# Two weight loads between the weightings of V, and V's last block weighted after all of them

## The chip, the cores and the metric

The kernel runs on one core of a Trainium2 chip. The metric is the device time of one execution in microseconds; lower is better. Three executions of the kernel before took 358.61 to 360.15 us, with a median of 359.97 us.

## What is computed

Eight batches of eight heads go through a causal attention whose scores decay with a running sum, and the result, rearranged to 4608 tokens of 512 numbers, goes through a normalised gated feed-forward layer:

```python
scores = scale * np.matmul(q, k.transpose(0, 1, 3, 2))
cum = np.cumsum(np.maximum(s, 0.0), axis=-1)
bias = -(cum[:, :, :, None] - cum[:, :, None, :])
scores = np.where(causal, -1000000000.0, scores + np.minimum(bias, 0.0))
attn = softmax(scores)                      # B, H, S, D = 8, 8, 576, 64
x = (attn @ v).transpose(0, 2, 1, 3).reshape(B * S, H * D)
xn = x / np.sqrt(np.mean(x * x, -1) + 1e-06) * rms_g
g, val = xn @ w_gate, xn @ w_val            # 512 x 1536 each
out = (g * sigmoid(g) * val) @ w_out        # 1536 x 512
```

## The kernel before

Everything is bf16 on TensorE (PE) with fp32 sums. A batch has 576 positions, in blocks of 128, 128, 128, 128 and 64. The feed-forward part works on nine chunks of 512 tokens. For each chunk, `ffn` (line 940) walks the 12 blocks of 128 hidden features, fb = 0 to 11: a product with `wg_sb` (line 957, here called G of block fb), one with `wv_sb` (line 967, V of block fb), ScalarE's tanh of G (line 960), two operations on VectorE (lines 970 and 962) that free the two PSUM banks again; then four blocks of tokens are multiplied by `wout_sb` (line 988). Between these products, `step` (line 855) deals out the attention of the next batches: transposes of K and Q (`t_step`, line 199, matmuls of line 203), scores (line 286), exponentials (lines 310 and 326), masks on GpSimd (line 319), the products with V (`av_step`, lines 437 and 443). Every engine executes its own instructions strictly in the order in which this code emits them; nothing reorders them later.

The change lies in the opening, written out by hand from line 1090 on, before the first chunk. There the attention of the first four blocks of batch 0 is done with nothing else beside it. The decay of batch 0 is folded into V: `fold_v` (line 415) multiplies one block of V by a number per row and head, on VectorE for block 1 and on GpSimd (POOL) for blocks 0, 2, 3 and 4. Block 4 of V is read by the last block's attention, which is dealt out only inside the first chunk.

The weights come in pieces by `load_w(src, dst, f0, f1)` (line 1007): a DMA that POOL issues, from fp32 in HBM to bf16 in SBUF, for the blocks f0 to f1-1. Before the change POOL issues them in this order: gate 0-3, val 0-1, then behind the three foldings val 2-5, after the last of the small normalisation operations (`alpha`, lines 474 and 477) gate 4-7 and val 6-11, and, out of the first chunk's steps, gate 8-11.

Two more things use the DMA engines and the same engines' queues at that time. `load1(g)` (line 1139) brings K and Q of batch 1 in fp32, four heads at a time: two DMAs of 512 KB each, issued by SyncE (SP), for heads 0-3 after the second block's attention and for heads 4-7 after the third's. They are turned into bf16 in pieces: K of heads 0-3 by four casts on VectorE (`piece1`, line 1255), Q of heads 0-3 by four on POOL (line 1253), K and Q of heads 4-7 half by POOL and half by ScalarE (lines 1265 to 1269). Only then can PE transpose them. The transposes stand in PE's order between the products of the first chunk: those of K, heads 0-3, ahead of G of block 2; the first of Q, heads 0-3, between G and V of block 2.

In the profile all weight loads have line 1009, all foldings on POOL line 417, the casts line 153 (POOL and VectorE) or 151 (ScalarE).

Of the kernel before, what the change touches and what calls it, by code (L numbers as in the profile page):

```python
# [26 lines left out]
def kernel(  # L27
# [34 lines left out]
    wg_sb = pers.tile([128, CC, DF], BF16, name="wg_sb")  # L62
    wv_sb = pers.tile([128, CC, DF], BF16, name="wv_sb")
# [45 lines left out]
    def psF():  # L109
        return pp.tile([128, DM], FP32, name="psF", tag="F", bufs=4)  # L110
# [304 lines left out]
    def fold_v(eng, c):  # L415

        eng.tensor_tensor(out=v_sb[:, 0, c], in0=v_sb[:, 0, c],
                          in1=vw[:, c, :].unsqueeze(2).to_broadcast([128, H, NV]), op=ALU.mult)
# [53 lines left out]
    def alpha(c0, c1, R=slice(0, 128)):  # L472

        nc.gpsimd.tensor_scalar(  # L474
            out=al_all[R, c0:c1], in0=ss_all[R, c0:c1],
            scalar1=1.0 / DM, scalar2=EPS, op0=ALU.mult, op1=ALU.add)
        nc.gpsimd.tensor_tensor(  # L477
            out=al_all[R, c0:c1], in0=al_all[R, c0:c1],
            in1=mhalf[R, 0:c1 - c0], op=ALU.pow)
# [369 lines left out]
    def warm(n):  # L849

        ps = psF()
        for i in range(n):
            nc.tensor.matmul(ps, lhsT=ident_bf, rhs=mneg, start=True, stop=True)
# [153 lines left out]
    def load_w(src, dst, f0, f1):  # L1007
        fs = slice(f0 * 128, f1 * 128)
        nc.gpsimd.dma_start(out=dst[:, :, fs],
                            in_=src[:, fs].rearrange("(cc p) f -> p cc f", p=128))  # L1010
# [79 lines left out]
    with tc.manual_schedule():  # L1090
# [32 lines left out]
        ACT, DVE, POOL = nc.scalar, nc.vector, nc.gpsimd  # L1123
# [4 lines left out]
        def pairF():  # L1128
            return (psF(), psF())

        def s_first(kb, g, pair=None):
            do_s((0, kb, g), pair)()
# [54 lines left out]
        s_first(2, 0)  # L1187
        fold_v(POOL, 0)
        load_w(moe_w_val, wv_sb, 0, 2)
        for c in (2, 3, 4):  # L1190
            fold_v(POOL, c)
        s_first(0, 1, pairF())
        tail_step(0, psAV16())
        fold_v(DVE, 1)
# [8 lines left out]
        norms += [do_av((0, 1, 1), psT32(), act=True, apart=True)]  # L1203
        norms[0](False)
        alpha(0, 1)
        load_w(moe_w_val, wv_sb, 2, 6)
        s_first(3, 1, pairF())
        norms[1](False)
        ps = psS()
# [13 lines left out]
        norms += [do_av((0, 3, 1), psT32(), act=True, apart=True)]  # L1223
        norms[3](False)
        alpha(3, 4)
        load_w(moe_w_gate, wg_sb, 4, 8)
        load_w(moe_w_val, wv_sb, 6, 12)
        warm(4)
        for qb in range(4):
            x_scale(0, qb, gq)  # L1230
# [253 lines left out]
```

## Time and profile before

| | |
|---|---|
| median of three executions | 359.97 us (358.61 to 360.15) |
| the profiled execution, its own time | 357.18 us |
| its span from first to last instruction | 355.7 us |
| granted TensorE clock over the span | 0.998 |
| PE busy | 343.4 us (97%) |
| VectorE (DVE) busy | 278.5 us (78%) |
| ScalarE (ACT) busy | 212.2 us (60%) |
| GpSimd (POOL) busy | 204.3 us (57%) |
| DMA, mean over the span | 128 GB/s |

Times in the rows of the trace are microseconds from the start of the span; the profiled execution's own time is 1.5 us more than the span. A row of the timeline has start, duration, engine, line, operation, what is written and read, and in brackets the idle time before it and what ended that. A row of the DMA view has the name of a queue, its packets, megabytes and the time that its packets took as a share of 16 engines over the window; queue q0 is that of the loads which POOL issues, q1 that of SP. A row of DMA issues ends with the microseconds from issue to landing.

### The profile page before, as it was taken

What the parts mean: (1) busy time and instruction counts of PE and PEld (TensorE: products, weight loads), DVE (VectorE), ACT (ScalarE), POOL (GpSimd) and SP (SyncE); (2) the same over time, 40 slices, a digit from 0 to 9 for tenths busy, and PEclk for the clock granted to TensorE, in tenths of its full rate; (3) what the DMA queues carried; (4) which work ended last, traced back from release to release, by engine and by line L of the source; (5) the groups of instructions that cost most, each with busy time, mean ns of one, the idle gap of its engine ahead of it and who ended that gap; (6) DMA issues with size and microseconds to landing.
All of it is one profiled execution on the core that took longest, in us unless ns stands there. A gap on an engine that the chain in (4) does not pass through costs nothing.

```text
span 355.7 us, 7020 instructions
## 1 busy us (share of the span) xinstructions
PE 343.4 (97%) x2461; PEld 167.4 (47%) x2461; DVE 278.5 (78%) x528; ACT 212.2 (60%) x467; POOL 204.3 (57%) x336
## 2 busy tenths in 40 slices
PE   5989999999999999999999999999999999999995
PEld 2465444544444444444454454444544554444443
DVE  6798889598967987798789886988798659836840
ACT  3977885878786546864577557654565445324322
POOL 6988564456669986687498988497735320000000
PEclk9999999999999999999999999999999999999999
DMA  7999999899959999999999999296810131020002
GB/s 217 145 241 235 172 178 260 188 192 199 92 122 170 147 149 155 166 206 181 154 150 132 79 151 198 38 105 103 153 24 17 46 104 23 2 88 29 2 32 92
DMA packets 130528, 45.68 MB, mean 128 GB/s; under 512 B 110548, under 2 KB 125656, under 8 KB 130488
## 3 DMA queue, kind: packets, MB, share of 16 engines
q0 software_dynamic: 67056, 13.70, 52.4%
q1 hardware_dynamic: 53792, 24.20, 35.4%
q10 hardware_dynamic: 9640, 7.29, 8.1%
q8 instruction: 20, 0.33, 0.5%
q14 instruction: 20, 0.16, 0.2%
HBM read 37.90 MB, written 9.44 MB: 133 GB/s over the span
## 4 chain that ended last, share of the span: by engine, by line
PE 77%; DMA 7%; POOL 4%; DVE 4%; ACT 3%; issue 3%; SPq 0%; POOLq 0%; DVEq 0%; ACTq 0%
PE psF L988 26%; PE psF L967 20%; PE psF L957 19%; DMA kqT<-kqn 4%; DMA wg_sb<-in_moe_w_gate_dram 3%; PE psAV L443 2%; PE psS L286 2%; PE psAV L437 2%; PE psF L367 1%; DVE U L970 1%; POOL v_sb L409 1%; PE psS L367 1%; DVE x_sb L453 1%; DVE Ht L962 1%; ACT E L326 1%
## 5 line engine op out<-in xcount | busy, mean ns | idle before, releaser
L957 PE MATMUL psF<-xnT,wg_sb 128*128 128x512 bf16 x424 | 108.9, 379 | 0.6 <-DMA wg_sb<-in_moe_w_gate_dram 0.5
L967 PE MATMUL psF<-xnT,wv_sb 128*128 128x512 bf16 x424 | 108.9, 379 | 0.4 <-DMA wv_sb<-in_moe_w_val_dram 0.4
L960 ACT ACTIVATE T<-psF 128x512 f32<-128x512 f32 x108 | 64.7, 599 | 64.5 <-PE psF L957 61.3
L988 PE MATMUL psF<-wout_sb,Ht 128*128 128x512 bf16 (+2 forms) x444 | 100.9, 374 | 0.0
L970 DVE SCALAR_TENSOR_TENSOR U<-T,psF 128x512 bf16<-128x512 f32 x108 | 73.6, 681 | 23.5 <-ACT T L960 23.1
L962 DVE TENSOR_TENSOR Ht<-U,psF 128x512 bf16<-128x512 bf16 x99 | 67.7, 684 | 6.8
L988 PEld LDWEIGHTS <-Ht 128*128 128x128 bf16 x444 | 40.1, 98 | 43.5 <-issue 1.4
L967 PEld LDWEIGHTS <-wv_sb 128*128 128x128 bf16 x424 | 38.9, 98 | 44.5 <-issue 2.9
L957 PEld LDWEIGHTS <-wg_sb 128*128 128x128 bf16 x424 | 38.6, 98 | 42.2 <-issue 1.9
L992 ACT ACTIVATE osb<-psF 128x512 f32<-128x512 f32 (+2 forms) x37 | 21.7, 586 | 59.5 <-PE psF L988 52.8
L384 POOL TENSOR_SCALAR_AFFINE_SELECT E<-E 128x512 bf16<-128x512 bf16 (+1 forms) x50 | 34.8, 704 | 29.5 <-ACT E L380 19.7
L194 POOL DMA_DIRECT2D v_sb<-in_v_dram x40 | 35.4, 885 | 0.2 <-issue 0.2
L484 DVE SCALAR_TENSOR_TENSOR xs_sb<-x_sb,al_all,g_row 128x512 bf16<-128x512 bf16 (+1 forms) x36 | 29.6, 821 | 4.1 <-POOL al_all L477 3.9
L310 ACT ACTIVATE E<-psS,biasK 128x256 bf16<-128x256 f32 (+3 forms) x88 | 29.3, 424 | 2.9 <-PE psS L286 2.9
L474 POOL TENSOR_SCALAR al_all<-ss_all 128x1 f32<-128x1 f32 (+2 forms) x39 | 11.5, 295 | 33.3 <-ACT xs_sb L461 26.9
L453 DVE TENSOR_TENSOR x_sb<-psAV,rZ 128x256 bf16<-128x256 f32 (+1 forms) x66 | 28.0, 424 | 2.3
L522 DVE TENSOR_TENSOR acc<-acc,mag 128x1280 bf16<-128x1280 bf16 x32 | 27.5, 878 | 0.2
L477 POOL TENSOR_TENSOR al_all<-al_all,mhalf 128x1 f32<-128x1 f32 (+2 forms) x39 | 25.2, 645 | 3.2
L443 PEld LDWEIGHTS <-E 128*128 128x128 bf16 x320 | 21.7, 98 | 10.5 <-POOL E L384 0.7
L409 POOL TENSOR_TENSOR v_sb<-v_sb,vwx 128x512 bf16<-128x512 bf16 x25 | 25.9, 1037 | 0.1
L461 ACT ACTIVATE xs_sb<-x_sb 128x512 bf16<-128x512 bf16 (+1 forms) x37 | 23.3, 629 | 4.3 <-DVE x_sb L453 3.7
L319 POOL TENSOR_SCALAR_AFFINE_SELECT E<-E 128x512 bf16<-128x512 bf16 x19 | 13.1, 691 | 19.2 <-ACT E L310 18.6
(141 smaller groups left out, 400.0 us busy)
## 6 DMA issues: line engine op xcount, KB each, us to landing
out_dram<-osb SPq DMA_DIRECT2D x35, 256.0 KB, 2.4
kq<-in_q_dram ACTq DMA_DIRECT2D x5, 1024.0 KB, 7.2
v_sb<-in_v_dram POOLq DMA_DIRECT2D x32, 128.0 KB, 5.6
kqn<-in_k_dram POOLq DMA_DIRECT2D x20, 128.0 KB, 4.9
kq<-in_k_dram SPq DMA_DIRECT2D x4, 512.0 KB, 5.6
kq<-in_q_dram SPq DMA_DIRECT2D x4, 512.0 KB, 7.4
wg_sb<-in_moe_w_gate_dram POOLq DMA_DIRECT2D x3, 512.0 KB, 10.4
wout_sb<-in_moe_w_out_dram POOLq DMA_DIRECT2D x2, 768.0 KB, 9.6
```

The source lines that it names most:

```text
L194: nc.gpsimd.dma_start(out=v_sb[0:n, b % 2, c, :, 0:64], in_=v[b, :, c * 128:c * 128 + n, :].rearrange("h p d -> p h d"))
L310: nc.scalar.activation(out=eo, in_=ei, func=AF.Exp, scale=0.125, bias=biasK[:, kb, bh:bh + 1])
L384: nc.gpsimd.affine_select(out=Ev, in_=Ev, pattern=[[0, 4], [1, nq]], compare_op=ALU.is_ge, fill=0.0, base=0, channel_multiplier=-1)
L409: nc.gpsimd.tensor_tensor(out=v_sb[:, b % 2, c, :, 0:64], in0=v_sb[:, b % 2, c, :, 0:64], in1=vwx[:, c, i:i + H].unsqueeze(2).to_broadcast ...
L453: nc.vector.tensor_tensor(out=xo[:, g * 256:(g + 1) * 256].rearrange("p (h d) -> p h d", h=4), in0=pv[R, :, 0:64], in1=rZ[R].unsqueeze(2). ...
L484: nc.vector.scalar_tensor_tensor(out=xs_sb[R, (b * NSC + qb) % NX, :], in0=x_sb[R, (b * NSC + qb) % NX, :], scalar=al_all[R, col:col + 1], ...
L957: nc.tensor.matmul(Gp, lhsT=wg_sb[:, cc, fs], rhs=xnT[:, cc, x0:x0 + DM], start=(cc == 0), stop=(cc == CC - 1))
L960: nc.scalar.activation(out=T, in_=Gp, func=AF.Tanh, scale=0.5)
L962: nc.vector.tensor_tensor(out=Ht[:, fb - 1, :], in0=pend[0], in1=pend[1], op=ALU.mult)
L967: nc.tensor.matmul(Vp, lhsT=wv_sb[:, cc, fs], rhs=xnT[:, cc, x0:x0 + DM], start=(cc == 0), stop=(cc == CC - 1))
L970: nc.vector.scalar_tensor_tensor(out=U, in0=T, scalar=1.0, in1=Gp, op0=ALU.add, op1=ALU.mult)
L988: nc.tensor.matmul(Op[:, p0:p1], lhsT=Ht[:, fb, tb * 128:(tb + 1) * 128], rhs=wout_sb[:, fb, p0:p1], start=(fb == 0), stop=(fb == FB - 1))
```

## The change

In the opening, val 2-5 and gate 4-7 are issued between the foldings: the order on POOL is now folding of block 2, load of val 2-5, folding of block 3, load of gate 4-7. The folding of block 4 moves from there to the end of the opening, behind the load of val 6-11, and so stands ahead of the casts of batch 1. The amount of work is the same.

```diff
         load_w(moe_w_val, wv_sb, 0, 2)
-        for c in (2, 3, 4):
-            fold_v(POOL, c)
+        fold_v(POOL, 2)
+        load_w(moe_w_val, wv_sb, 2, 6)
+        fold_v(POOL, 3)
+        load_w(moe_w_gate, wg_sb, 4, 8)
         s_first(0, 1, pairF())
...
         alpha(0, 1)
-        load_w(moe_w_val, wv_sb, 2, 6)
         s_first(3, 1, pairF())
...
         alpha(3, 4)
-        load_w(moe_w_gate, wg_sb, 4, 8)
         load_w(moe_w_val, wv_sb, 6, 12)
+        fold_v(POOL, 4)
         warm(4)
```

The first place is POOL's order from the folding of block 0 on. In these rows line 417 is a folding, line 1009 a weight load (128x4x256 has two blocks of features, 128x4x512 four, 128x4x768 six), lines 474 and 477 are the two operations of `alpha`. Before:

```order
L417 TENSOR_TENSOR v_sb<-v_sb,vw 128x520
L1009 DMA wv_sb<-in_moe_w_val_dram 128x4x256
L417 TENSOR_TENSOR v_sb<-v_sb,vw 128x520 x3
L474 TENSOR_SCALAR al_all<-ss_all 128x1
L477 TENSOR_TENSOR al_all<-al_all,mhalf 128x1
L1009 DMA wv_sb<-in_moe_w_val_dram 128x4x512
L474 TENSOR_SCALAR al_all<-ss_all 128x2
L477 TENSOR_TENSOR al_all<-al_all,mhalf 128x2
```

The same place now:

```order
L417 TENSOR_TENSOR v_sb<-v_sb,vw 128x520
L1009 DMA wv_sb<-in_moe_w_val_dram 128x4x256
L417 TENSOR_TENSOR v_sb<-v_sb,vw 128x520
L1009 DMA wv_sb<-in_moe_w_val_dram 128x4x512
L417 TENSOR_TENSOR v_sb<-v_sb,vw 128x520
L1009 DMA wg_sb<-in_moe_w_gate_dram 128x4x512
L474 TENSOR_SCALAR al_all<-ss_all 128x1
L477 TENSOR_TENSOR al_all<-al_all,mhalf 128x1
L474 TENSOR_SCALAR al_all<-ss_all 128x2
```

Val 2-5 has moved ahead of two foldings and the first `alpha`, gate 4-7 ahead of all `alpha` operations, and one folding is gone from here.

The second place is POOL's order at the end of the opening, where line 153 is the casts of Q of batch 1, heads 0-3, and line 319 a mask of the last block's scores of batch 0. Before:

```order
L474 TENSOR_SCALAR al_all<-ss_all 128x1
L477 TENSOR_TENSOR al_all<-al_all,mhalf 128x1
L1009 DMA wg_sb<-in_moe_w_gate_dram 128x4x512
L1009 DMA wv_sb<-in_moe_w_val_dram 128x4x768
L153 COPY kqn<-kq_75 128x256 x4
L1009 DMA wg_sb<-in_moe_w_gate_dram 128x4x512
L319 AFFINE_SELECT E<-E 128x8x64
```

And now:

```order
L474 TENSOR_SCALAR al_all<-ss_all 128x1
L477 TENSOR_TENSOR al_all<-al_all,mhalf 128x1
L1009 DMA wv_sb<-in_moe_w_val_dram 128x4x768
L417 TENSOR_TENSOR v_sb<-v_sb,vw 128x520
L153 COPY kqn<-kq_75 128x256 x4
L1009 DMA wg_sb<-in_moe_w_gate_dram 128x4x512
L319 AFFINE_SELECT E<-E 128x8x64
```

One load has gone from in front of the casts, and a folding has come. On PE, ACT, DVE and SP the order of instructions is the same as before.

## The prediction

> **What bounds the kernel now.** I read the page's busy shares first, then the chain of work that ended last, then the waits of PE in the opening.
>
> ```profile
> PE 343.4 (97%) x2461; PEld 167.4 (47%) x2461; DVE 278.5 (78%) x528; ACT 212.2 (60%) x467; POOL 204.3 (57%) x336
> PE 77%; DMA 7%; POOL 4%; DVE 4%; ACT 3%; issue 3%; SPq 0%; POOLq 0%; DVEq 0%; ACTq 0%
> ```
>
> PE is busy 97% of the span and makes up 77% of the chain. A microsecond that PE stands still in the first chunk is therefore a microsecond on the total, in either sign: nothing later has room to take it back. The waits of PE before 80 us that name a weight are these:
>
> ```profile
> PE psF L957 <- DMA wg_sb<-in_moe_w_gate_dram: 0.5, 1, 0.5
> PE psF L967 <- DMA wv_sb<-in_moe_w_val_dram: 0.4, 1, 0.4
> ```
>
> So 0.9 us is all that earlier weights can give back directly. That is 0.25% of the time. What they may cost must be looked for in the things that share POOL and the DMA engines with them.
>
> **POOL's side of the change.** The rows of POOL around the moved instructions, from its timeline:
>
> ```profile
> 16.15 0.80 POOL L1009 DMA_DIRECT2D wv_sb<-in_moe_w_val_dram  x1
> 16.98 3.51 POOL L417 TENSOR_TENSOR v_sb<-v_sb,vw 128x520 bf16<-128x520 bf16 x3
> ...
> 21.37 0.84 POOL L1009 DMA_DIRECT2D wv_sb<-in_moe_w_val_dram  x1
> 22.57 0.18 POOL L474 TENSOR_SCALAR al_all<-ss_all 128x2 f32<-128x2 f32 x1 [0.36 <-ACT xs_sb L461]
> ...
> 24.57 0.81 POOL L1009 DMA_DIRECT2D wg_sb<-in_moe_w_gate_dram  x1
> 25.38 0.78 POOL L1009 DMA_DIRECT2D wv_sb<-in_moe_w_val_dram  x1
> 26.82 1.85 POOL L153 CAST kqn<-kq 128x256 bf16<-128x256 f32 x4 [0.66 <-DMA kq<-in_q_dram]
> 28.62 0.74 POOL L1009 DMA_DIRECT2D wg_sb<-in_moe_w_gate_dram  x1
> ```
>
> A folding takes 3.51 / 3 = 1.17 us, an issue about 0.8. Now the first folding ends at 16.98 + 1.17 = 18.15, val 2-5 is issued there instead of at 21.37 (3.2 us earlier), the second folding ends near 20.1, and gate 4-7 is issued there instead of at 24.57 (4.5 us earlier). The first alpha starts near 20.9 instead of 20.5, and is over before the one at 22.57, which waits for ACT in any case. After the third alpha, val 6-11 is issued at 24.57, 0.8 us earlier, and the folding of block 4 runs from 25.4 to 26.5. That is before 26.82, when the casts started because Q had landed. So on POOL itself **the edit costs nothing**: the loss of cover would show only if Q landed sooner than before.
>
> Block 3 is weighted 0.8 us later, at 20.1. Its reader on PE is here, and it waited for something else:
>
> ```profile
> 21.16 0.20 PE L437 MATMUL psAV<-v_sb,E 128*128 128x65 bf16 x1 [0.49 <-DVE g_col L1213]
> ```
>
> That leaves a microsecond. Block 4 is needed by the attention of the last block, inside the first chunk and behind G of block 2 at 29.55 (row further down); 26.5 is early enough. Both at nothing.
>
> **The DMA side.** Here the loads meet those of K and Q of batch 1. SP's issues, then the landings:
>
> ```profile
> 19.67 0.39 SPq L137 DMA_DIRECT2D kq<-in_k_dram  x1
> 20.22 0.86 SPq L137 DMA_DIRECT2D kq<-in_q_dram  x1
> 21.81 0.37 SPq L137 DMA_DIRECT2D kq<-in_k_dram  x1
> ```
>
> ```profile
> kq<-in_k_dram SPq DMA_DIRECT2D x1, 512.0 KB, 5.6
> kq<-in_q_dram SPq DMA_DIRECT2D x1, 512.0 KB, 6.5
> wv_sb<-in_moe_w_val_dram POOLq DMA_DIRECT2D x1, 256.0 KB, 7.6
> wv_sb<-in_moe_w_val_dram POOLq DMA_DIRECT2D x1, 512.0 KB, 9.9
> wg_sb<-in_moe_w_gate_dram POOLq DMA_DIRECT2D x1, 512.0 KB, 10.4
> ```
>
> K of heads 0-3 landed at 19.67 + 5.6 = 25.3, Q at 20.22 + 6.5 = 26.7, val 0-1 at 16.15 + 7.6 = 23.8, val 2-5 at 31.3, gate 4-7 at 35.0. Who used the DMA engines in between shows in the queues, window by window: 18 to 20 us, 22 to 23, 23 to 25, 25 to 26, 26 to 31.
>
> ```profile
> q0 software_dynamic: 297, 0.29, 108.9%
> ...
> q1 hardware_dynamic: 239, 0.24, 80.9%
> ...
> q1 hardware_dynamic: 670, 0.67, 97.5%
> q0 software_dynamic: 12, 0.01, 3.2%
> ...
> q0 software_dynamic: 32, 0.03, 20.0%
> ...
> q0 software_dynamic: 590, 0.59, 69.1%
> q1 hardware_dynamic: 646, 0.64, 46.2%
> ```
>
> This is the heart of it. From 22 to 25 us the queue of POOL was almost empty, and SP's K and Q had the engines to themselves: 670 packets of 1 KB in 2 us, 335 a microsecond. Once weights were there too (26 to 31), the engines were just as full, and SP's queue got 646 / 5 = 129 packets a microsecond, POOL's 118. **The hole in POOL's queue was no idle time: K and Q filled it.** The change closes it. Val 2-5 and gate 4-7 are now both in the queue by 20.9, directly behind val 0-1, and from about 22 on K and Q have to share.
>
> By 25.0, SP's queue had moved 239 + 670 = 909 packets in 3 us; K and Q of heads 0-3 together are 1024. At 129 a microsecond the 909 take 7.0 us, so Q lands 4.0 us later and K, the first half of them, 2.0 us later: 30.7 and 27.3. To that comes the time that a queue needs to get in beside a busy one. Val 2-5, whose issue ended at 22.2, joined a busy SP queue and had 12 packets up to 25.0: some 2.8 us. The other order (SP's queue joining a busy POOL queue) isn't shown past 22; the ends are 0 and 2.8. I take 0.5, near the lower end, because SP's queue, issued from 19.67 on behind a POOL queue that had stood at 108.9%, was at 80.9% by 22 to 23. So **K at 27.8, Q at 31.2**, heads 4-7 of K another 512 / 129 = 4.0 us behind, at 35.2.
>
> The Trainium skill, in DMA: Bandwidth & Descriptors, section Queues, rings and completion order, says that each DMA engine takes turns between its queues, a packet of several descriptors at a time. The even split of 590 and 646 agrees, and it speaks against this change: by that rule what the weights gain, K and Q lose, and the sum stays the one below.
>
> **What waits for K and Q.** DVE, PE and ACT rows of the timeline:
>
> ```profile
> 25.58 1.08 DVE L153 CAST kqn<-kq 128x256 bf16<-128x256 f32 x4
> 26.57 0.81 DVE L516 TENSOR_SCALAR mag<-kqn 128x2560 uint16<-128x2560 uint16 x1
> 28.27 0.69 DVE L970 SCALAR_TENSOR_TENSOR U<-T,psF 128x512 bf16<-128x512 f32 x1 [0.88 <-ACT T L960]
> ```
>
> ```profile
> 29.55 1.03 PE L957 MATMUL psF<-xnT,wg_sb 128*128 128x512 bf16 x4
> 30.51 0.38 PE L203 MATMUL psT<-ident_bf,kqn 128*128 128x128 bf16 x4
> 31.28 1.04 PE L967 MATMUL psF<-xnT,wv_sb 128*128 128x512 bf16 x4 [0.39 <-DMA wv_sb<-in_moe_w_val_dram]
> ...
> 35.01 1.04 PE L957 MATMUL psF<-xnT,wg_sb 128*128 128x512 bf16 x4 [0.50 <-DMA wg_sb<-in_moe_w_gate_dram]
> ```
>
> ```profile
> 31.76 0.77 ACT L151 ACTIVATE kqn<-kq 128x256 bf16<-128x256 f32 x2
> 32.58 0.60 ACT L211 ACTIVATE kqT<-psAV 128x512 bf16<-128x512 bf16 x1
> 33.44 0.60 ACT L960 ACTIVATE T<-psF 128x512 f32<-128x512 f32 x1 [0.27 <-PE psF L957]
> 36.08 0.60 ACT L960 ACTIVATE T<-psF 128x512 f32<-128x512 f32 x1 [2.05 <-PE psF L957]
> ```
>
> *K late.* DVE's casts move from 25.58 to 27.8, 2.2 us; 0.88 of it is idle time ahead of 28.27, so U is 1.3 us late and ends near 30.3. G of block 2 at 29.55 reuses the bank that U frees, and starts near 30.3. This delay lies inside the next one.
>
> *Q late.* POOL's casts run from 31.2 to 31.2 + 1.85 = 33.05. The transpose at 30.51 reads them, so it starts at 33.05, **2.5 us late**, and all of PE's queue behind it: V of block 2, the products of block 3, the attention of the last block. POOL's next load issue takes 0.74 us, so its mask for that attention starts near 33.8, and PE comes to it only just ahead of G of block 4, near 36.
>
> *Val and gate early.* They have landed before, so the waits of 0.39 and 0.50 us are gone. From the transpose to G of block 4 there were 35.01 - 30.51 = 4.5 us, now 3.6. **G of block 4 starts at 36.65, 1.6 us late.**
>
> *K of heads 4-7 late.* ACT's cast moves from 31.76 to 35.2, 3.4 us, and the tanh behind it ends at 35.2 + 0.77 + 0.60 + 0.60 = 37.2. But ACT had 2.05 us of idle time before 36.08, and its next tanh now needs G of block 4, done at 36.65 + 1.04 = 37.7. That is covered, with 0.5 us to spare.
>
> The sum is 2.5 - 0.9 = **+1.6 us**: 357.18 becomes 358.8 for the profiled execution. The median of the runs lies 2.8 us over that execution; the same shift gives 359.97 + 1.6 = **361.6 us**.
>
> **The rivals.**
>
> *K and Q lose more.* If SP's queue gets in only after 2.8 us, Q lands at 33.5, the transpose starts at 35.35, 4.8 us late, and less 0.9 that is +3.9: 363.9 us. It is the same mechanism at its upper end. For it speaks how long val 2-5 stood outside a busy queue; against it, that SP's queue was at 80.9% from 22 on, a time at which POOL's last load, val 0-1, had not yet landed. By the same page's rule a queue may empty a whole packet first, which would lie between my value and this one.
>
> *Not slower: K and Q keep their pace.* If Q still lands by 30.51 - 1.85 = 28.7, that is no more than 2.0 us late instead of 4.5, the transpose doesn't move and the two waits vanish: -0.9, 359.1 us. This decides at a rate for SP's queue of about 909 / (3 + 2) = 180 packets a microsecond instead of 129. Against it speaks the row of 26 to 31 us, for it that the two queues together might move more where the weights are still few. The section Anatomy of one DMA of the same page fits a load as 2.0 us and its bytes at 436 GB/s, so 3.2 us for 512 KB, an estimate by which the weights would be through before they can disturb; the 9.9 and 10.4 us above disagree.
>
> *It doesn't do what it says.* POOL's queue is in order, and val 0-1 lands only at 23.8; if the issue wasn't what held val 2-5 back, it lands as before, K and Q too: 0, 360.0 us. The 12 packets from 23 to 25 us speak against that.
>
> **How the numbers follow.** The forecast, sharing at the measured rate, gets 0.58, and its own range is 361.1 to 363.0 (0 and 1.9 us for getting in). The bound of 0.5%, about what a measurement of this kernel can tell from no change, is 1.8 us, so I split it: 0.31 within, 0.27 slower. K and Q losing more: 0.19, slower. K and Q at their pace: 0.18; 0.9 us is within the bound, but the sum may hide a second stall that goes, so 0.08 faster and 0.10 within. No effect: 0.05, within. Together faster 0.08, within 0.46, slower 0.46. The range runs from 359.1, the end of the third case, to 363.9, the upper end of the second.
>
> **What would show it.** In the new profile, q1 should have about 130 packets a microsecond between 23 and 25 instead of 335, and q0 as many. POOL's casts at 26.82 should wait for Q until about 31, the transpose on PE wait for POOL, and no wait for a weight should be left. If the casts start before 28.7, the forecast is wrong and the gain is near 0.9 us. If ACT waits for its cast past 35.7, the cover of the last point is gone, and the loss is larger than the sum.

## The result, and the profile after

Five executions of the changed kernel took 363.73 to 364.99 us, with a median of 364.43; five of the kernel before, on the same chip, had a median of 358.84. The ratio is 1.0149, with a 95% interval of 1.0115 to 1.0183: about 5.5 us slower, past the upper end of the range. The forecast, 361.6 us, stood 1.6 us above the 359.97 of before that it started from. (Ratios here leave out runs over 1.5% above the fastest of their kernel, among them three of the ten of the late casts below; medians don't.) The profiled execution took 364.09 us with a span of 362.6, 6.9 us more than that of before.

The page of the changed kernel: the busy times and the chain of work by engine, to be held against the two lines for before in the prediction, and TensorE's granted clock in 40 slices, with that of before behind it.

```profile
PE 343.6 (95%) x2416; PEld 168.0 (46%) x2461; DVE 278.8 (77%) x528; ACT 212.7 (59%) x467; POOL 204.7 (56%) x336
PE 72%; DMA 11%; POOL 7%; DVE 4%; issue 3%; ACT 1%; SPq 1%; POOLq 0%; DVEq 0%; ACTq 0%
PEclk9999799999999999999999999999999999999999
```

```profile
PEclk9999999999999999999999999999999999999999
```

No engine is busy for noticeably longer. DMA has grown from 7 to 11% of the chain, POOL from 4 to 7%, and the fifth slice, 36 to 45 us, ran at 0.7 of the clock. PE's waits before 80 us that are new:

```profile
PE psT L203 <- POOL kqn L153: 2.9, 2, 2.2
PE psF L957 <- DVE U L970: 0.9, 1, 0.9
```

The two waits for weights are gone. In their place PE waits 2.9 us, in two pieces, for POOL's casts of Q, and 0.9 for U. SP's issues of K and Q, and then the landings of K, Q, val 2-5 and gate 4-7 (the last number, us from issue):

```profile
19.46 0.39 SPq L137 DMA_DIRECT2D kq<-in_k_dram  x1
20.00 1.14 SPq L137 DMA_DIRECT2D kq<-in_q_dram  x1
```

```profile
kq<-in_k_dram SPq DMA_DIRECT2D x1, 512.0 KB, 9.2
...
kq<-in_q_dram SPq DMA_DIRECT2D x1, 512.0 KB, 13.6
...
wv_sb<-in_moe_w_val_dram POOLq DMA_DIRECT2D x1, 512.0 KB, 10.3
...
wg_sb<-in_moe_w_gate_dram POOLq DMA_DIRECT2D x1, 512.0 KB, 12.7
```

K lands at 28.7 (before 25.3) and Q at 20.00 + 13.6 = 33.6 (before 26.7). The weights, issued at 18.44 and 20.27, are there at 28.7 and 33.0 and no longer matter. The two queues in the windows 20 to 22 us, 23.25 to 23.5, 23 to 25, 25 to 31 and 31 to 34 (packets, MB, share):

```profile
q0 software_dynamic: 523, 0.32, 125.0%
...
q1 hardware_dynamic: 15, 0.02, 22.1%
...
q0 software_dynamic: 292, 0.28, 83.4%
q1 hardware_dynamic: 201, 0.21, 35.5%
...
q0 software_dynamic: 696, 0.76, 72.8%
q1 hardware_dynamic: 712, 0.71, 42.7%
...
q1 hardware_dynamic: 292, 0.28, 35.0%
```

The same of before, SP's queue in the windows 21.25 to 21.5, 20 to 22 and 25 to 26:

```profile
q1 hardware_dynamic: 5, 0.01, 6.4%
...
q1 hardware_dynamic: 44, 0.05, 14.2%
...
q1 hardware_dynamic: 290, 0.29, 87.6%
```

POOL's queue no longer runs empty. SP's queue has its first packets between 23.25 and 23.5 us, though K was issued at 19.46; before, they came between 21.25 and 21.5. From 25 on it gets 712 / 6 = 119 packets a microsecond beside POOL's 116. Now those who wait for K and Q: POOL, DVE, PE.

```profile
25.34 1.06 POOL L417 TENSOR_TENSOR v_sb<-v_sb,vw 128x520 bf16<-128x520 bf16 x1
33.72 2.02 POOL L153 CAST kqn<-kq 128x256 bf16<-128x256 f32 x4 [7.31 <-DMA kq<-in_q_dram]
```

```profile
28.63 0.90 DVE L153 CAST kqn<-kq 128x256 bf16<-128x256 f32 x4 [3.06 <-DMA kq<-in_k_dram]
```

```profile
30.92 1.02 PE L957 MATMUL psF<-xnT,wg_sb 128*128 128x512 bf16 x3 [0.87 <-DVE U L970]
34.17 0.57 PE L203 MATMUL psT<-ident_bf,kqn 128*128 128x128 bf16 x2 [2.23 <-POOL kqn L153]
35.45 0.63 PE L203 MATMUL psT<-ident_bf,kqn 128*128 128x128 bf16 x2 [0.70 <-POOL kqn L153]
35.87 1.91 PE L967 MATMUL psF<-xnT,wv_sb 128*128 128x512 bf16 x4
...
41.74 1.03 PE L957 MATMUL psF<-xnT,wg_sb 128*128 128x512 bf16 x4
```

V of block 2 starts at 35.87 instead of 31.28, 4.6 us late, and G of block 4 at 41.74 instead of 35.01, 6.7 us late. So 2.1 us are lost behind the wait, with nothing to wait for, although the 0.50 us for gate 4-7 is saved there. The rows tell why: four products of 512 columns take 1.91 us where they took 1.04. The granted clock is the number behind POOL's busy time in the windows of 34 to 42 us, the third from the right:

```profile
34.00:35.00 1.00, 0.46 (x2) 0.19 (x2) 1.00 (x2) 0.00 (x0) 1.00 (x3) 0.88 1.10 279
...
40.00:41.00 1.00, 1.00 (x4) 0.31 (x3) 0.41 (x1) 0.56 (x1) 1.00 (x2) 0.50 1.35 188
41.00:42.00 1.00, 1.00 (x12) 0.60 (x11) 0.33 (x2) 0.00 (x0) 0.89 (x3) 0.71 2.15 142
```

From 35 to 41 us it is 0.50. With the parts of the windows on both sides, (1.00 - 0.88) / 0.5 + 6 + (1.00 - 0.71) / 0.5 = 6.8 us ran at half clock. Before, the clock is 1.00 over all of 30 to 42 us.

### The profile page after: what moved, and what is told of

The parts are those of the page before. It is cut to its first block, busy times and chain, and to the rows that moved or that the text cites. A ratio compares the mean times of both kernels' runs of the same rounds, so it can differ in the third digit from the quotient of the medians.

```text
span 362.6 us, 6975 instructions
## 1 busy us (share of the span) xinstructions
PE 343.6 (95%) x2416; PEld 168.0 (46%) x2461; DVE 278.8 (77%) x528; ACT 212.7 (59%) x467; POOL 204.7 (56%) x336
## 4 chain that ended last, share of the span: by engine, by line
PE 72%; DMA 11%; POOL 7%; DVE 4%; issue 3%; ACT 1%; SPq 1%; POOLq 0%; DVEq 0%; ACTq 0%
PE psF L988 24%; PE psF L967 20%; PE psF L957 19%; DMA kq<-in_q_dram 5%; DMA kqT<-kqn 5%; PE psAV L443 2%; POOL v_sb L194 2%; PE psS L286 1%; PE psAV L437 1%; PE psF L367 1%; DVE U L970 1%; POOL kqn L153 1%; DVE Ht L962 1%; PE psS L367 1%; POOL v_sb L417 1%
## 5 line engine op out<-in xcount | busy, mean ns | idle before, releaser
L957 PE MATMUL psF<-xnT,wg_sb 128*128 128x512 bf16 x406 | 107.6, 382 | 1.9 <-DVE U L970 0.9
L988 PE MATMUL psF<-wout_sb,Ht 128*128 128x512 bf16 (+2 forms) x428 | 98.9, 373 | 1.4 <-issue 0.8
L443 PEld LDWEIGHTS <-E 128*128 128x128 bf16 x320 | 21.8, 98 | 10.6 <-POOL E L384 0.7
L437 PEld LDWEIGHTS <-E 128*128 128x128 bf16 x256 | 20.1, 98 | 8.2 <-DVE x_sb L453 1.3
```

The source lines that it names most:

```text
L443: nc.tensor.matmul(o, lhsT=d, rhs=v_sb[:, p, qb, h, :], start=(j == 0 and qb == 0), stop=(j == 3))
L957: nc.tensor.matmul(Gp, lhsT=wg_sb[:, cc, fs], rhs=xnT[:, cc, x0:x0 + DM], start=(cc == 0), stop=(cc == CC - 1))
L988: nc.tensor.matmul(Op[:, p0:p1], lhsT=Ht[:, fb, tb * 128:(tb + 1) * 128], rhs=wout_sb[:, fb, p0:p1], start=(fb == 0), stop=(fb == FB - 1))
```

## The experiments

Four theories were put against each other. **A**: POOL's queue is never empty when K and Q come, so SP's queue gets in late and then shares. **B**: only the bytes ahead of Q count, each moved load costing its own share. **C**: it is POOL's order, the folding of block 4 ahead of the casts. **D**: a part of the loss is the half clock that follows PE's standstill, and goes with it.

**The folding alone.** The kernel before, with only the folding of block 4 moved.

```diff
-        for c in (2, 3, 4):
+        for c in (2, 3):
             fold_v(POOL, c)
...
         load_w(moe_w_val, wv_sb, 6, 12)
+        fold_v(POOL, 4)
```

> Only the folding of V's block 4 moves behind the load of val 6-11; all loads stay where they were. Theory A (POOL's queue no longer runs empty when K and Q of batch 1 come): no weight is in the queue earlier, so Q lands near 26.7 us and the time is that of before within 1 us. Theory B (the loss is the bytes that stand ahead of Q): the same. Theory C (the folding in front of the casts of Q holds up POOL): the casts start over 1 us late and the time is 1 to 5 us over that of before.

Measured: 359.57 us against 358.62, ratio 1.0011 (0.9987 to 1.0034). The casts of Q start at 27.81 us instead of 26.82, and no transpose waits for them. The edit also brings the issue of val 2-5 forward, from 21.37 to 20.70, and Q lands at 20.17 + 7.5 = 27.7; the folding had ended at 27.3, so the later start of the casts isn't its doing. C falls: the folding is free, as forecast.

**Each load alone, and both.** The kernel before with val 2-5 moved, with gate 4-7 moved, and with both but all foldings left where they stood. The core of the diffs (the later calls are taken out accordingly; the first has only the first load, the second only the second):

```diff
-        for c in (2, 3, 4):
-            fold_v(POOL, c)
+        fold_v(POOL, 2)
+        load_w(moe_w_val, wv_sb, 2, 6)
+        fold_v(POOL, 3)
+        load_w(moe_w_gate, wg_sb, 4, 8)
+        fold_v(POOL, 4)
```

> Only val 2-5 is issued earlier, between the foldings; gate 4-7 and the folding of block 4 stay. Theory A: val 2-5 keeps the queue busy until gate 4-7 is in it at its old place, so SP's queue gets in as late and shares as long as with both loads moved: Q lands near 33, the transpose waits over 3 us, and the whole loss is there, +5 to +6 us. Theory B: half of the bytes ahead of Q, so Q lands near 30 and the loss is 1 to 3 us.

> Only gate 4-7 is issued earlier, between the foldings of blocks 3 and 4; val 2-5 stays behind the first normalisation. Theory A: POOL's queue holds gate 4-7 and then val 2-5 without a gap, Q lands near 33 again, +5 to +6 us; val 2-5 lands behind gate 4-7, near 33, but PE is held by Q by then. Theory B: half of the loss, 1 to 3 us, and a wait of PE for val 2-5 on top.

> Both loads are issued between the foldings, the folding of block 4 stays there too, behind gate 4-7. Theories A and B: the time of the changed kernel, 5 to 6 us over before, since the folding's place costs nothing. Theory C: no folding stands in front of the casts any more, so the time is within 1 us of before.

Measured, all against 358.62: val alone 362.50, ratio 1.0111 (1.0086 to 1.0135); gate alone 363.56, 1.0159 (1.0124 to 1.0194); both 364.29, 1.0175 (1.0138 to 1.0213). Either load alone makes most of the loss, and the second adds little. By its time, val alone lies between the 1 to 3 us of B and the 5 to 6 us of A. Q's landing tells more: 12.1 us after its issue with val alone, 11.7 with gate alone, 13.3 with both, and 6.5 before. B, in which the two delays add, doesn't fit. The queues show that they do it in two ways. With val alone, in the windows 23 to 24, 25 to 28 and 23 to 28 us:

```profile
q0 software_dynamic: 202, 0.19, 115.5%
q1 hardware_dynamic: 25, 0.03, 9.2%
...
q1 hardware_dynamic: 1002, 1.00, 96.8%
q0 software_dynamic: 72, 0.06, 12.8%
...
q1 hardware_dynamic: 1169, 1.17, 69.8%
```

SP's queue gets in as late as with both loads, but has the engines nearly to itself from 25 on. With gate alone, in the windows 22 to 23 and 24 to 28, it is the other way round:

```profile
q1 hardware_dynamic: 218, 0.22, 66.2%
...
q0 software_dynamic: 469, 0.47, 73.0%
q1 hardware_dynamic: 444, 0.45, 39.9%
```

SP's queue gets in on time (218 packets; before 239), and then has to share: 444 packets in 4 us are 111 a microsecond. Val 2-5 keeps it out, gate 4-7 takes two thirds of its pace (111 of 335). The casts of Q start at 32.2 us in both, at 33.7 with both loads. One thing in the first doesn't fit A: the 1169 packets that SP's queue had by 28 us are more than the 1024 of K and Q, yet the casts waited for Q until 32.16. The counts are sums over 16 engines; that one engine was far behind is likely, but no row here shows it.

The run with both loads shows one thing more. PE waits there for POOL's casts as in the changed kernel (2.15 and 0.77 us), but its granted clock in the windows 35 to 36, 36 to 38 and 38 to 40 us is this:

```profile
35.00:36.00 1.00, 0.35 (x3) 0.23 (x4) 0.21 (x1) 0.00 (x0) 1.00 (x3) 0.84 1.10 306
36.00:38.00 2.00, 2.00 (x9) 0.90 (x9) 0.09 (x1) 0.60 (x1) 1.19 (x2) 0.50 1.02 253
38.00:40.00 2.00, 2.00 (x10) 0.94 (x9) 0.59 (x1) 1.53 (x4) 1.50 (x4) 0.73 1.20 219
```

The half clock lasts 0.32 + 2 + 1.08 = 3.4 us, half as long as the 6.8 us in the changed kernel's profile, behind much the same standstill. With gate alone it is 3.4 us too, with val alone 6.8.

**The standstill filled.** The changed kernel with 14 products ahead of the first transpose of Q on PE. Nobody reads their sum.

```diff
     def do_t(key, **kw):
         b, hp, w = key
+        if key == (1, 0, 1):
+            stir(14)
```

> The changed kernel with 14 products of 128x512 on TensorE, whose sums nobody reads, put ahead of the first transpose of Q, so that PE works (about 3 us) where it otherwise stands still. Theory D (part of the loss is the half clock that PE is granted after it has stood still): the granted clock stays at 1.0 from 32 to 42 us, the products behind the transpose take 1.03 us for four instead of 1.91, and the time falls by 2 to 3 us against the changed kernel, to 2 to 4 us over before. Rival (the half clock comes from something else, or the whole loss is Q's lateness): the added work lies inside the wait and the time stays 5 to 6 us over before, or rises.

Measured: 361.06 us against 358.38, ratio 1.0075 (1.0051 to 1.0099). PE's timeline (lines past 688 are two higher):

```profile
32.20 3.19 PE L1151 MATMUL psAV<-mneg,ident_bf 128*128 128x512 bf16 x14
...
35.85 0.58 PE L203 MATMUL psT<-ident_bf,kqn 128*128 128x128 bf16 x2 [0.36 <-POOL kqn L153]
36.27 1.03 PE L969 MATMUL psF<-xnT,wv_sb 128*128 128x512 bf16 x4
```

POOL's casts start at 33.53, as late as in the changed kernel, and V of block 2 at 36.27, even later. But the products behind it take 1.03, the clock over the span is 1.000, and half of the loss is gone. The ten executions had mean clocks of 0.994 to 1.000, the five of the changed kernel 0.986 to 0.990. **3.2 us of useless work on PE made the kernel some 2.7 us faster** (0.74% of 358.4): D holds.

**K and Q issued earlier.** The changed kernel with `load1(0)` moved ahead, behind VectorE's folding.

```diff
         fold_v(DVE, 1)
+        load1(0)
...
         do_av((0, 1, 0))
-        load1(0)
```

> The changed kernel with K and Q of heads 0-3 of batch 1 issued about 1.9 us earlier, behind VectorE's folding of block 1 (near 17.7 us), ahead of val 2-5. Theory A (what counts is which queue is in first, and how long SP's queue shares): SP's packets start near 21 instead of 23, Q lands near 31.5 instead of 33.6, the transpose waits 2 us less, and the time is 2 to 4 us below the changed kernel; gate 0-3 or val 0-1 may land up to 1 us late. Theory C (POOL's order): no difference from the changed kernel.

Measured: 361.68 us against 358.38, ratio 1.0090 (1.0053 to 1.0126). The first transposes of Q, in PE's timeline:

```profile
31.48 0.23 PE L203 MATMUL psT<-ident_bf,kqn 128*128 128x128 bf16 x1 [0.94 <-POOL kqn L153]
32.41 0.57 PE L203 MATMUL psT<-ident_bf,kqn 128*128 128x128 bf16 x2 [0.71 <-POOL kqn L153]
33.75 0.23 PE L203 MATMUL psT<-ident_bf,kqn 128*128 128x128 bf16 x1 [0.76 <-POOL kqn L153]
33.81 1.03 PE L967 MATMUL psF<-xnT,wv_sb 128*128 128x512 bf16 x4
```

Issued 1.7 us earlier (17.76), Q lands 2.7 us earlier, at 30.9: its queue, too, gets in earlier, with 52 packets before 22 us, which is what A says. But POOL's queue wasn't empty then: it moved 82 packets between 21.25 and 21.5 us, when SP's had its first two, 3.5 us after the issue. That fits a delay by the loads issued ahead better than a delay until POOL's queue runs empty; no run here shows the reason. PE waits nearly as long as in the changed kernel (2.4 us for POOL), but in three pieces with transposes between, and the clock of the profiled execution stays at 1.00. That isn't so in every execution: three of the seven had 1.00, the others 0.991 to 0.995. Of the 3.7 us by which the profiled span is over that of before, V of block 2 makes 2.5, and a wait of 1.07 us at 42.45 for ACT, whose casts had waited for Q of heads 4-7, most of the rest.

**Who else can come late.** The kernel before, with K and Q of heads 4-7 issued after the weights instead of ahead of them.

```diff
-        load1(1)
         norms[2](False)
...
             x_scale(0, qb, gq)
+        load1(1)
```

> The kernel before, with K and Q of heads 4-7 issued only behind the scalings of x on VectorE (near 25.7 us instead of 21.8). Theory A: val 2-5 then has the engines for itself from 25 to 27 and lands near 29, gate 4-7 near 33.5; both waits of PE for weights vanish, -0.5 to -0.9 us, and K and Q of heads 4-7 land 1 to 2 us later, which ACT's and POOL's idle time covers. Rival: K of heads 4-7 comes too late for ACT's cast, and the time rises by 1 to 3 us.

Measured: 362.96 us against 358.38, ratio 1.0110 (1.0071 to 1.0148). In PE's timeline:

```profile
38.06 0.21 PE L437 MATMUL psAV<-v_sb,E 128*128 128x65 bf16 x1 [4.00 <-ACT kqT L211]
...
38.47 1.90 PE L957 MATMUL psF<-xnT,wg_sb 128*128 128x512 bf16 x4
```

Both waits for weights are gone here as well, but ACT waits 4.52 us for K of heads 4-7, PE 4.00 us for ACT behind it, and the next product runs at half clock, which lasts 3.4 us here. The loss is larger than the 1 to 3 us of the rival. Heads 4-7 have slack, as the prediction had it, but not this much: whoever is issued behind the weights pays for them.

**A quarter of val 2-5.** The kernel before, with 128 rows of val 2-5 issued between the foldings and the other 384 at their old place.

```diff
+        fold_v(POOL, 2)
+        load_part(moe_w_val, wv_sb, 2, 6, 0, 1)
+        fold_v(POOL, 3)
+        fold_v(POOL, 4)
...
-        load_w(moe_w_val, wv_sb, 2, 6)
+        load_part(moe_w_val, wv_sb, 2, 6, 1, 4)
```

> The kernel before, with a quarter of val 2-5 (128 of its 512 packets) issued between the foldings of blocks 2 and 3 and the other three quarters at their old place. Theory B (bytes ahead of Q): 128 packets are about 0.9 us of POOL's queue, Q lands near 27.6, inside its slack: within 1 us of before. Theory A (the queue must run empty for SP's queue to get in): the quarter delays SP's first packets by about 1 us, and Q lands 1 to 3 us late, for a loss of 0 to 1.5 us.

Measured: 359.38 us against 358.38, ratio 1.0029 (0.9995 to 1.0063). Q landed 7.5 us after its issue, at 27.8 instead of 26.7; no transpose waited. A and B had both forecast this, so the run doesn't decide between them. The delay grows with what stands in POOL's queue when K and Q are issued, and the first 2.0 us of it are free: until 30.51 - 1.85 = 28.7 us nobody waits for Q.

**A standstill without the loads.** The kernel before, with no load or folding moved; POOL does the four casts of Q four times over, each time with the same values.

```diff
-        piece1(POOL, 1, 0, 0, 4)
+        for i in range(4):
+            piece1(POOL, 1, 0, 0, 4)
```

> The kernel before, with none of the loads or foldings moved, but POOL does the four casts of Q of batch 1, heads 0-3, four times over (each time with the same result), 12 casts more than needed. A cast takes 0.46 us, so the last one ends near 26.8 + 4 x 1.85 = 34.2 us instead of 28.7, and PE's transpose at 30.5 waits for POOL until then, 3.7 us late, about as late as in the changed kernel (34.17). K, Q and the weights land when they did. If a half clock follows whenever PE stands still in this way (theory D), the products behind the transpose run at half clock from about 35 us for some 6 us and the time is 358.6 + 3.7 - 0.9 (both weight waits are covered) + 2.6, about 364.0. If the half clock in the changed kernel came from something in the loads, the clock stays at 1.00 and the time is near 361.4.

Measured: median 362.14 us against 358.50, ratio 1.0067 (1.0028 to 1.0106). PE's wait, and the granted clock from 33 to 35 and 40 to 41 us:

```profile
PE psT L203 <- POOL kqn L153: 3.5, 1, 3.5
```

```profile
33.00:34.00 1.00, 0.00 (x0) 0.00 (x0) 0.77 (x2) 0.00 (x0) 1.00 (x3) 0.96 1.15 240
34.00:35.00 1.00, 0.51 (x2) 0.21 (x2) 0.00 (x0) 0.00 (x0) 1.00 (x4) 0.50 1.22 228
...
40.00:41.00 1.00, 1.00 (x7) 0.36 (x5) 0.69 (x1) 0.24 (x1) 1.00 (x3) 0.63 1.36 169
```

The half clock is there with the loads untouched: it needs only the standstill. Its length is 0.08 + 6 + 0.74 = 6.8 us. This execution has a second half clock, of 3.4 us from 177.3 on, behind a wait of PE of 1.29 us for a transposing DMA (`kqT<-kqn`), which helps to put it above the 364.0 expected. And the half clock isn't there in every execution. The ten runs reach from 359.34 us at a mean granted clock of 0.999 to 365.79 at 0.986, which is the profiled one; three of them had 0.998 or more and took 359.3 to 361.1. The median lies between the 364.0 expected with the half clock and the 361.4 without. So the mechanism is shown by the rows of one execution and by the clocks of the others, but its price holds only for the executions that meet it, and for as long as it lasts in them. The five of the changed kernel all had 0.986 to 0.990.

**Both remedies.** The changed kernel with the 14 products and the earlier issue of K and Q.

> The changed kernel with both remedies: load1(0) issued behind the folding on VectorE, and 14 idle products on PE ahead of the first transpose of Q (their sum is read by nobody). If what POOL's busy queue costs (theory A) and what the half clock costs (theory D) are two separate terms, Q lands near 31, the casts end near 33, the idle products are wholly or mostly inside PE's wait, and the time lies near that of the earlier issue alone, 361.7, since that one already ran at full clock: 361.0 to 361.9. If the remedies added up in full (each took 2.7 to 3.2 us from the changed kernel) it would be near 358.5, the time of the kernel before.

Measured: 360.72 us against 358.50, ratio 1.0060 (1.0025 to 1.0096), just below the lower end for two separate terms. The remedies don't add up, since with the earlier issue alone the clock of the profiled execution was at 1.00 already; with the filler as well, nine of ten executions had 0.998 or more, against three of seven without. PE's products ended near 35.1 while POOL's casts ended at 33.3, so that some of what is left is the filler itself. No version tried was faster than the kernel before.

## Why the prediction was wrong, point by point

Two steps failed. The delay of Q was set too small, above all the time that SP's queue needs to get in (0.5 us taken, 2.0 measured), and PE's wait was priced at its length alone, without the half clock behind it (2.6 us). The points in the prediction's order:

- **What can be won.** Right: the two waits of 0.5 and 0.4 us are gone, and nothing else came back.
- **POOL's side of the change, blocks 3 and 4.** Right: the folding of block 4 lies inside the idle time ahead of the casts (25.34, casts at 33.72), and moved alone it changed nothing that can be measured (1.0011).
- **K and Q fill the hole in POOL's queue, and lose it.** Right in mechanism, too small in size. The forecast had Q 4.5 us later: 4.0 by sharing at 129 packets a microsecond and 0.5 for getting in beside a busy queue. Measured: 6.9 us. This can be split by counting. After, 201 + 712 = 913 of the 1024 packets had gone by 31 us; the other 111, at 292 / 3 = 97 a microsecond, end at 32.1. From 23.4 on that is 8.7 us, 118 packets a microsecond. Before, 44 had gone by 22 us, the 909 of the forecast by 25, and the last 71, at 290 a microsecond, by 25.2: 3.8 us from 21.4 on. So sharing cost 8.7 - 3.8 = 4.9 us, and **getting in 23.4 - 21.4 = 2.0 us instead of 0.5**. That is the first step that failed: I took the low end of 0 to 2.8 us, and the row on which I leaned (SP's queue at 80.9% by 22 to 23 us) belonged to the very situation that the change removes, a POOL queue about to run empty. The rate was a smaller miss, 129 against 118.
- **K late.** Right in kind: K at 28.7 instead of the 27.8 forecast, U 1.9 us late, G of block 2 at 30.92 instead of 30.3, all inside the wait for Q.
- **Q late.** Forecast: transpose 2.5 us late. Measured: V of block 2 started 4.6 us late with its own wait of 0.39 gone, so 5.0. The first rival, with 4.8 us and Q at 33.5, described this step almost to the number, partly by luck: it had 2.8 us for getting in and 4.0 for sharing, where 2.0 and 4.9 were measured. The forecast chose wrongly between two ends of one mechanism.
- **From there to G of block 4.** Forecast 0.5 us shorter, because gate 4-7 is there. It was: but at half clock, 35.87 to 41.74 took 5.87 us instead of 31.28 to 35.01, 3.73. Without the 0.50 us it would have been 3.23, so **the half clock cost 2.6 us. No step of the prediction and no rival had it.** PE's waits were priced at their length, as if the work behind them ran on as before: that is the second step that failed. The 2.6 us are those of this execution; with both loads, where the half clock lasted 3.4 us, V of block 2 to G of block 4 took 40.56 - 35.95 = 4.61, so 1.4 more than 3.23.
- **K of heads 4-7.** Right for the changed kernel, but for another reason: ACT's cast started at 37.28, past the 35.7 that was named as the limit of the cover, but PE was later still. Where PE ran at full clock it wasn't covered: in the profiles with the filler and with the earlier issue, PE waits 0.46 and 0.49 us for ACT's copy behind that cast.

```profile
37.28 0.72 ACT L151 ACTIVATE kqn<-kq 128x256 bf16<-128x256 f32 x2 [0.57 <-DMA kq<-in_k_dram]
...
42.81 0.60 ACT L960 ACTIVATE T<-psF 128x512 f32<-128x512 f32 x1 [2.25 <-PE psF L957]
```

The sum, with the measured terms: 5.0 + 2.6 - 0.9 = 6.7 us at G of block 4 (41.74 - 35.01 = 6.73), and 6.9 in the span. The medians differ by less, 5.6. The causes are shown by taking them away: the filler leaves Q late and removes the half clock (1.0149 becomes 1.0075), the earlier issue leaves the weights early and removes part of the delay (1.0090), though some of that gain is the clock, which was 1.00 in three of its seven executions. Why Q's last packets came so late with val 2-5 alone stays open.

The Trainium skill, in TensorE: Matmul & The Clock Gate, section Part 1: The HAM clock gate, says that TensorE's clock drops to half after an idle window of about 3.4 us, that the window runs freely, so that the outcome varies from run to run, and that about 3.4 us of work brings the clock back. The runs agree with the drop, with the variation (359.34 to 365.79 us for one kernel) and with the length: the half clock lasted 3.4 us in three of the profiles above and twice that, 6.8 us, in three others. They differ in what it takes. PE needn't stand still for 3.4 us on end: the changed kernel's standstill was two pieces of 2.23 and 0.70 us, with two transposes between, and with val 2-5 alone the clock fell at 32.6 us, when PE had stood still for 1.3 us.

## What to carry to other kernels

A hole in one DMA queue may be the time in which another does its work: before moving a load ahead, look at who fills the hole, and count a full delay for getting in beside a busy queue besides the rate of sharing, here a third (119 of 335 packets a microsecond). A wait on an engine that is busy 97% of the time can cost more than its length, since the work behind it may run at half clock. In the profiles here that followed waits of 2.6 to 4.0 us for POOL or ACT, and didn't follow one of 2.4 us in three pieces. Filling the wait kept the clock up. That breaking it up would do is not shown: with val 2-5 alone it came in pieces of 1.31, 0.65 and 0.70 us, and the clock fell in the first. The loads moved here could give back 0.9 us at most, and the loads that they displaced had 2.0 us of slack: that comparison alone speaks against the change.

## What was not expected of the hardware

- A queue that joins a busy one stays outside for long: SP's K was issued at 19.46 us and had its first packets after 23.25, 3.8 us later; with POOL's queue about to run dry, 19.67 to 21.25, some 1.6 us.
- Two queues together move fewer packets than one alone: 119 + 116 = 235 a microsecond between 25 and 31 us, against 335 for SP's queue alone before. POOL's packets are the slower ones: alone, between 18 and 20 us before, that queue moved 297 in 2 us, 149 a microsecond, so a mix of the two must lie in between, and the row alone doesn't show that sharing itself costs anything.
- Products that nobody needs can pay: 14 of them took 3.19 us of PE's time and made the kernel faster, by keeping the clock at 1.00.
- The half clock behind a standstill comes in two lengths, 3.4 and 6.8 us, in the profiles of kernels that differ little and of waits of much the same length. It also came without the late Q: with the folding alone, the clock was 0.50 from 172 to 175 us, behind a wait of 1.37 us for `kqT<-kqn`; before, PE waited 0.87 us there and the clock stayed at 1.00.
